# Where the first products of the second chunk's weights and the first maxima rows stand around a guard's branch

## The chip, the cores and the metric

The kernel runs on one core of a Trainium2 chip. The metric is the device time of one execution in microseconds (us); the time given for a kernel is the median of its runs. The profile is of one execution, taken by the hardware profiler; its times count from the first instruction. PE is the matrix engine (PEld its weight loads), DVE the vector engine, ACT the scalar engine, POOL the general one; SP only starts transfers here. A letter q behind an engine's name marks its instruction sequencer.

## The reference

One token block of 2048 rows and 512 columns goes through a layer norm; the result xn feeds two branches, and both are added to x.

```python
q = (xn @ wq) split in 32 heads of 16;  k = xn @ wk;  v = xn @ wv      # one shared key and value head
A = softmax(q k^T / 4) v, heads joined, @ wo

qB = einsum("nd,dhc->nhc", xn, w_q)                                  # 32 heads, 2 x 128 columns
s1, s2 = qB[..., :128] @ k1^T, qB[..., 128:] @ k2^T                     # 64 scores each
the two best of s1 and of s2 -> the two best of their four sums -> experts top_e, gates g
B = sum over heads and both experts of g * gelu(xn . u[top_e]) * v[top_e]   # 4096 experts
out = x + A + B
```

## The kernel before

The 32 expert heads are taken in 8 chunks of 4, the 2048 rows in 4 blocks of 512. For a chunk c, `wp_make(c)` (line 477) joins the query weights with the keys k1 and k2, so that one product with xn gives the scores: per head the raw weights are loaded by `wp_load(c, h)` (line 466), multiplied by the keys on PE into `pw` (line 487) and copied by ACT into `wt` (line 488); then four times four transposes `pwt` (line 494), a rounded high part by ACT (line 496) and the rest by DVE (line 497) make the tiles `wk`. `item` (line 513) multiplies them with xn into `psc` (line 531) and DVE finds the best entries. Blocks 0 and 1 then gather their experts' rows from HBM (`gather`, line 976, by POOL; `dot` and `add` on DVE); blocks 2 and 3 compute all experts densely (`dense`, line 656).

The attention runs in 32 units of four heads and 512 rows. `load_q(u)` (line 305) fills one of two tiles `qa`: for each of two pairs of heads three transfers of query rows, and one (line 314) of two rows of maxima, `d_m`, that are subtracted through the score product. `scores` (line 323) multiplies with the keys into `sc`, ACT takes the exponential into `pt` (line 330), and `pv` (line 338) multiplies by the values.

The maxima are normally zeros, which `zero_m` writes early. `guard` (line 251) bounds the largest score: DVE takes maxima, PE turns them (`pm`, line 258), DVE reduces, multiplies and compares (lines 260 to 264). Each engine then loads the flag into a register (line 265) and branches (line 266): only if the flag is set does `true_maxima` (line 269) compute the true ones. With these inputs it isn't set, and the block, which holds thousands of instructions, is jumped over.

Everything up to and including the guard is ordered by the framework's scheduler, which takes instructions by priority (their order in the program) as they become ready. The projections of this part use the pool `start`; when they are traced, `start_stack.close()` gives its space back and the pool `late` is opened in it (line 1251): the tiles `pt`, `e`, and the three buffers with the tag `gy`, which also take the raw weights from the third head of chunk 1 on. Buffers for the raw weights of that chunk's first two heads stand outside (lines 1249, 1250).

Behind the guard the order on every engine is written by hand. A loop over d (line 1259) calls `att_steps` for two of the 512 attention steps at a time: scores, values, `mid()` for the expert work of DVE and ACT, scores again, and `fill()`. `fill` draws work from the generator `score_thread` by `run_scores` (line 1130), which runs pieces and adds each one's planned cost to `spent[0]`, until a target is reached: 0.9 for a head's products (line 489), 0.45 for four transposes (line 500), three times `UNIT` (0.705) for a quarter of an item. The target of iteration d is line 1324. In the first iteration `att_steps` also loads the maxima rows of unit 0 and draws work ahead of the first scores (lines 1156 to 1158).

```python
aim = done0 + (FILL - done0) * (d + 1) / half if d < half else 1e6      # FILL 948, half 256
```

Of the kernel before, what the change touches and what calls it, by code (L numbers as in the profile page):

```python
# [49 lines left out]
HOLD = 44  # L50
MOST = 4.0
UNIT = 0.235


@with_exitstack
def tile_kernel(ctx, tc, x, wq, wkv, wo, wqT, kT, uv, ub, vb, out):
# [194 lines left out]
    def guard():  # L251

        mm = small.tile([P, 2], F32, name="mm", bufs=1)
        nc.vector.reduce_max(mm[:, 0:1], qmax, axis=AX.X)
        nc.vector.reduce_max(mm[:, 1:2], ksq_p, axis=AX.X)
        p = xtile("pm")
        for i in range(2):
            nc.tensor.transpose(p[:1, i * P:(i + 1) * P], mm[:, i:i + 1], ident)
        m2 = small.tile([1, 2], F32, name="m2", bufs=1)
        nc.vector.reduce_max(m2, p[:1, :2 * P].rearrange("p (a n) -> p a n", a=2), axis=AX.X)  # L260
        pr = small.tile([1, 1], F32, name="prd", bufs=1)
        nc.vector.tensor_mul(pr, m2[:, 0:1], m2[:, 1:2])
        fl = small.tile([1, 1], I32, name="flag", bufs=1)
        nc.vector.tensor_scalar(fl, pr, LIMIT2, None, op0=OP.is_gt)
        flag = nc.values_load(fl[0:1, 0:1], min_val=0, max_val=1)
        with tc.If(flag != 0):
            true_maxima()

    def true_maxima():
        ptile = lambda dt, shape: late[0].tile(list(shape), dt, name="mx", tag="pt", bufs=6)  # L270
# [34 lines left out]
    def load_q(u, rows=True, maxima=True):  # L305
        qb, hg = units[u]
        qa = qa_bufs[u % 2]
        QA[u] = qa
        c = slice(qb * 512, (qb + 1) * 512)
        for b in range(2):  # L310
            h0 = 4 * hg + 2 * b
            o = 64 * b
            if maxima:
                nc.sync.dma_start(raw(qa[o + 48:o + 50]), d_m[:, h0:h0 + 2, c])
            if rows:
                src = [d[h0 * DH:(h0 + 2) * DH, c].rearrange("(h r) n -> r h n", r=DH) for d in (d_qh, d_ql)]
                nc.sync.dma_start(raw(qa[o:o + 16]), src[0])
                nc.sync.dma_start(raw(qa[o + 16:o + 32]), src[0])
                nc.sync.dma_start(raw(qa[o + 32:o + 48]), src[1])
# [193 lines left out]
    def item(n_, ti, make=()):  # L513
# [15 lines left out]
        for k in range(KC):  # L529
# [6 lines left out]
            if k < KC - 1:  # L536
                yield 3 * UNIT
            if k == 1:
# [8 lines left out]
        if jb == BT - 1:  # L547
            batch(ph, c, b)
        yield 3 * UNIT

# [105 lines left out]
    def dense(DG, after):  # L656
# [81 lines left out]
        def first(b):  # L738
            p = xtile("pact")
            for k in activations(b, early[b], p):  # L740
                if k < KC - 1:
                    yield 3 * UNIT
            g, y = gate_rows(b), hh[:, b, :]
# [8 lines left out]
            LATER.append(go)  # L752
            yield 3 * UNIT

# [107 lines left out]
        def sums():  # L862
# [4 lines left out]
            for j in range(GT):  # L867
# [7 lines left out]
                nc.vector.tensor_add(acc, acc, p)  # L875
                yield 6 * UNIT

# [250 lines left out]
    spent = [0.0]  # L1128

    def run_scores(until=None, key=None):  # L1130
        while (until is not None and spent[0] < until) or (key is not None and key not in IDX):
            posts()
            try:
                cost = next(sgen)
            except StopIteration:
                spent[0] = 1e9
                posts()
                return
            if cost is None:

                if key is None:
                    return
                continue
            spent[0] += cost
# [4 lines left out]
    def att_steps(d, mid, fill):  # L1149
        i = 2 * d  # L1150
        run(STORES)
        if 144 <= i < STEPS and i % 128 == 16:
            PWO.extend((i // 128 - 1, j) for j in range(4))
        if i < STEPS:
            u, kc = divmod(i, 16)
            if i == 0:
                load_q(0, rows=False)
                run_scores(until=spent[0] + 1.8)
            if kc == 4 and u + 1 < 32:
                load_q(u + 1)  # L1160
            scores(u, kc, 0)
            scores(u, kc, 1)
        if 0 < i <= STEPS:
            pu, pk = divmod(i - 2, 16)
            pv(pu, pk)
            pv(pu, pk + 1)
            if pk == 14:
                unit_tail(pu)
        mid()
        if i < STEPS:  # L1170
            scores(u, kc + 1, 0)
            scores(u, kc + 1, 1)
        if out_ready() and (i % 128 >= HOLD and PWO[0][0] != 1 or i % 128 >= 32 and i % 4 == 0 and PWO[0][0] == 1):
            block_out()
            spent[0] += 3.6
        fill()

        pp, r = divmod(i, 32)
        if pp and pp < 16:
            if r == 4:  # L1180
                pair_load(pp - 1)
            if r == 6:
                pair_invert(pp - 1)
            if r == 10:
                pair_spread(pp - 1)
            if r == 12:
                pair_tail(pp - 1)
        if STEPS - 4 <= i <= STEPS:
            last_out_a((i - STEPS) // 2 + 2)
        if i == STEPS:  # L1190
            last_out_a(3)
        if i == STEPS + 2:
            last_out_b()
        if i >= 124 and i % 128 == 124 or i == STEPS - 30:
            lent[0] = 2
        if 128 <= i < STEPS and i % 128 == (26 if i // 128 == 2 else 10) or i == STEPS - 10:
            load_wo()
        if i == STEPS - 6:
            load_last()
# [49 lines left out]
    wp_load(1, 0)  # L1249
    wp_load(1, 1)  # L1250
    late[0] = pool("late", bufs=1)
    load_q(0, maxima=False)
    guard()
    E_ = mybir.EngineType
    with tc.manual_schedule(engines={E_.PE, E_.Activation, E_.DVE, E_.Pool, E_.SP}):
        done0 = spent[0]
        half = STEPS // 2
        pos, since = 0.0, half
        for d in range(half + 24):


            if dense_on[0] != 0:
                since = d
            if dense_on[0] == 1:
                pos += 2.6 if d < half * 3 // 4 else max(0.0, NSL - pos) / max(half - 3 - d, 1)
            else:
                pos += (2.1 if len(IDX) < NC * TPH else 2.3 if 0 <= d - since < 12 else 1.75, 0, 1.4, 1.5, 0.5)[dense_on[0]]

            todo = max(min(int(pos + 0.001), g_next[0]) - d_next[0], 0)

            def mid():
                post = POST[:]
                POST.clear()
                for act, _ in post:
                    act()
                tanhs(d_next[0])
                run(ON_ACT)
                ON_ACT.extend(LATER_ACT)
                LATER_ACT.clear()
                run(LAST)  # L1280
                LAST.extend(LATER)
                LATER.clear()
                rest = BEHIND[:]
                BEHIND.clear()

                dots(d_next[0] + todo - 1)
                if a_ready[0] > a_next[0]:
                    weigh(a_next[0] // SB)
                dots(d_next[0] + 1 if todo > 0 else 0)
                for _, fn in post:  # L1290
                    fn()
                sums = min(a_ready[0] - a_next[0], max(todo, 3) if d < half else 4)
                if dense_on[0] > 2:
                    sums = min(sums, 2)
                if quiet[0] > 0:
                    quiet[0] -= 1
                    sums = 0
                if dense_on[0] == 2:
                    run(CHAIN)

                def go():
                    n = sums
                    while rest or CHAIN or n > 0:
                        if n > 0:
                            adds(1)
                            n -= 1
                        elif not rest:
                            run(CHAIN)
                        if CHAIN:
                            CHAIN.pop(0)()  # L1310
                        if rest:
                            rest.pop(0)()
                    gathers(4)

                    for _ in range(1 if d < half - 4 else NT):
                        if OUTS:
                            experts_out(OUTS.pop(0))

                if dense_on[0] == 2:
                    POST_FILL.append(go)  # L1320
                else:
                    go()

            aim = done0 + (FILL - done0) * (d + 1) / half if d < half else 1e6

            def fill():
                run_scores(until=min(aim, spent[0] + MOST))
                run(POST_FILL)

            att_steps(d, mid, fill)  # L1330
        flush()
        run(STORES)
        while a_next[0] < NSL:
            dots(NSL)
            run(CHAIN)
            tanhs(d_next[0])
            adds(SB)
            run(STORES)
            gathers(NGB)
        assert not OUTS  # L1340
        run(STORES)
# [37 lines left out]
```

## Time and profile before

| | us |
|---|---|
| median of 3 runs (1899.36, 1899.49, 1910.27) | 1899.49 |
| the profiled execution, device time | 1905.66 |
| its span, first to last instruction | 1903.9 |

PE is busy in 95% of the span, DVE in 86%, ACT in 68%, POOL in 37%. In rows of the timeline the columns are the start, the duration, the engine, the line, the operation, the tiles written and read, the count of merged instructions, and in brackets the idle time before and who ended it. A duration of merged rows is that of the whole row. Rows of a group view give the shortest, the median and the longest duration in ns, and the first and last start. Rows of stretches give the stretch, its length, each engine's busy time with its number of instructions, the granted PE clock, the share of the DMA engines and GB/s.

### The profile page before, as it was taken

How to read it: one execution, taken by the hardware profiler on the slowest of the kernel's cores; microseconds unless marked ns; L12 is line 12 of the kernel's file. 1: busy time of each engine (PE TensorE's matmuls, PEld its weight loads, DVE VectorE, ACT ScalarE, POOL GpSimd, SP SyncE). 2: the span in 40 equal slices, each digit the busy share in tenths (PEclk: the TensorE clock that was granted, in tenths of full speed). 3: DMA queues.
4: the chain of work that ended last, by engine and by line, in shares of the span. 5: the costliest groups of instructions: out<-in, count | busy, mean ns of one | idle time of the engine just before them, and what ended most of it. 6: DMA issues, size and time to landing. Idle time of an engine off the chain costs nothing.

```text
span 1903.9 us, 35010 instructions
## 1 busy us (share of the span) xinstructions
PE 1817.4 (95%) x10990; PEld 957.9 (50%) x10990; DVE 1632.6 (86%) x6381; ACT 1290.6 (68%) x1803; POOL 697.3 (37%) x920
## 2 busy tenths in 40 slices
PE   6879999999999899999999999999998899999998
PEld 4544444555555344555555554555543355555553
DVE  6627788889998987999999898899989879999994
ACT  3236666655557887877887555555579877888874
POOL 1202334334443213344444345344532134444430
PEclk9989999999999999999999999999999999999999
DMA  7857878888773678799899987877736878899883
GB/s 267 318 187 245 287 264 299 290 291 284 233 264 102 222 234 264 250 282 294 269 284 301 371 290 246 289 247 262 240 111 227 263 224 291 274 281 289 275 278 102
DMA packets 245724, 489.76 MB, mean 257 GB/s; under 512 B 93972, under 2 KB 106644, under 8 KB 245532
## 3 DMA queue, kind: packets, MB, share of 16 engines
q0 software_dynamic: 73728, 268.47, 42.6%
q1 hardware_dynamic: 170568, 218.18, 35.0%
q8 instruction: 88, 1.44, 0.3%
q10 hardware_dynamic: 1236, 0.82, 0.1%
q14 instruction: 104, 0.85, 0.1%
HBM read 426.49 MB, written 55.61 MB: 253 GB/s over the span
## 4 chain that ended last, share of the span: by engine, by line
PE 74%; DVE 11%; DMA 3%; ACT 3%; issue 2%; SPq 0%; DVEq 0%; ACTq 0%; POOL 0%; POOLq 0%
PE pv L341 20%; PE psc L531 17%; PE sc L327 15%; PE pact L733 9%; PE pout L872 9%; DVE oh L792 3%; PE pwo L434 2%; DVE xa L1034 2%; DVE g L999 2%; ACT pt L330 2%; PE pw L487 2%; DMA wk<-dw 1%; DVE oh L795 1%; DVE i L546 1%; DVE oh L794 1%
## 5 line engine op out<-in xcount | busy, mean ns | idle before, releaser
L330 ACT ACTIVATE pt<-sc 128x1024 f32<-128x1024 f32 x1024 | 994.5, 1028 | 435.2 <-PE sc L327 384.7
L987 POOL DMA_INDIRECT g<-in_uv_dram,idx x512 | 559.0, 1092 | 988.9 <-DVE xa L1034 517.1
L341 PE MATMUL pv<-pt,vaug 128*32 128x512 f32 x4096 | 498.9, 605 | 0.0
L327 PE MATMUL sc<-qa,kaug 64*128 64x512 f32 x2048 | 388.4, 451 | 17.9 <-ACT pt L330 15.9
L531 PE MATMUL psc<-wk,xt 128*128 128x512 f32 x1536 | 388.9, 401 | 4.2 <-DVE wk L497 3.6
L1034 DVE SCALAR_TENSOR_TENSOR xa<-g,w,xa 128x512 f32<-128x512 f32 x512 | 372.5, 746 | 0.1
L999 DVE CUSTOM_DVE_ANT_0 g<-g,xa 128x512 f32<-128x512 f32 x512 | 336.0, 683 | 8.7 <-DMA g<-in_uv_dram,idx 8.3
L531 PEld LDWEIGHTS psc<-wk,xt 128*128 128x128 f32 x1536 | 277.7, 188 | 107.9 <-issue 41.2
L327 PEld LDWEIGHTS sc<-qa,kaug 64*128 64x128 f32 x2048 | 157.4, 185 | 335.5 <-ACT pt L330 218.2
L341 PEld LDWEIGHTS pv<-pt,vaug 128*32 128x32 f32 x4096 | 107.6, 110 | 246.8 <-issue 246.8
L546 DVE FIND_INDEX8 i<-m,psc 128x8 uint32<-128x64 f32 x1024 | 206.6, 223 | 0.0
L733 PE MATMUL pact<-xt,wk 128*128 128x512 f32 x768 | 195.9, 400 | 0.0
L872 PE MATMUL pout<-wk,wd 128*128 128x512 f32 x768 | 194.9, 402 | 0.2 <-DVE wd L930 0.2
L544 DVE MAX8 m<-psc 128x8 f32<-128x64 f32 x1024 | 146.7, 216 | 35.8 <-PE psc L531 28.3
L872 PEld LDWEIGHTS pout<-wk,wd 128*128 128x128 f32 x768 | 140.8, 188 | 47.5 <-DVE act L999 5.1
L733 PEld LDWEIGHTS pact<-xt,wk 128*128 128x128 f32 x768 | 139.4, 188 | 48.5 <-issue 17.5
L875 DVE TENSOR_TENSOR da<-da,pout 128x512 f32<-128x512 f32 x128 | 83.0, 681 | 9.9 <-PE pout L872 9.8
L698 DVE TENSOR_TENSOR wk<-rw,wk 128x512 fp32r<-128x512 f32 x128 | 85.0, 685 | 6.7 <-ACT wk L697 6.7
L792 DVE TENSOR_TENSOR oh<-oh 128x2048 f16<-128x2048 f16 x64 | 78.0, 1219 | 0.6 <-issue 0.4
L697 ACT CAST wk<-rw 128x512 fp32r<-128x512 f32 x128 | 74.1, 631 | 0.0
L546 DVE MATCH_VALUE_LOAD i<-m,psc 128x8 f32 x1024 | 73.8, 72 | 0.0
L590 POOL CAST fi<-i 128x64 f32<-128x64 uint32 x32 | 8.9, 278 | 148.9 <-DVE i L546 148.2
(159 smaller groups left out, 1350.0 us busy)
## 6 DMA issues: line engine op xcount, KB each, us to landing
wk<-dw SPq DMA_DIRECT2D x96, 512.0 KB
wqt<-in_wqT_dram SPq DMA_DIRECT2D x32, 512.0 KB
dw<-wk SPq DMA_DIRECT2D x32, 512.0 KB
rw<-in_ub_dram SPq DMA_DIRECT2D x64, 256.0 KB
rw<-in_vb_dram SPq DMA_DIRECT2D x64, 256.0 KB
gy<-dg SPq DMA_DIRECT2D x64, 256.0 KB
qa<-dqh SPq DMA_DIRECT2D x128, 64.0 KB
g<-in_uv_dram,idx POOLq DMA_INDIRECT x512
```

The source lines that it names most:

```text
L327: nc.tensor.matmul(p[:, b, :], kaug[o:o + 64, kc * P:(kc + 1) * P], QA[u][o:o + 64, i, :], start=True, stop=True)
L330: nc.scalar.activation(pt, p, AF.Exp, scale=SCALE)
L341: nc.tensor.matmul(PV[u][32 * j:32 * j + 32, :], vaug[:, kc, :], pt[:, b, :], start=kc == 0, stop=kc == 15)
L531: nc.tensor.matmul(p, XT[k][:, a, j * P:(j + 1) * P], WC[n_][k][:, bb, :], start=n == 0, stop=n == 11)
L544: nc.vector.max(m8[:, jb, s, :], p[:, s * E:(s + 1) * E])
L546: nc.vector.max_index(i8[:, jb, s, :], m8[:, jb, s, :], p[:, s * E:(s + 1) * E])
L733: nc.tensor.matmul(p, us[:, a, k * P:(k + 1) * P], XT[k][:, c, :], start=n == 0, stop=n == 11)
L792: nc.vector.tensor_tensor(out=oa, in0=num(P), in1=bc(0, tb, P), op=OP.is_equal)
L872: nc.tensor.matmul(p, wd[0][:, a, j * P:(j + 1) * P], vs[:, c, :], start=n == 0, stop=n == 5)
L987: nc.gpsimd.indirect_dma_start(out=gt, out_offset=None, in_=uv, in_offset=bass.IndirectOffsetOnAxis(ap=IDX[ph, c, ti][:, s:s + 1], axis=0))
L999: nc.vector.tensor_tensor_reduce(u, u, XN[TPH * ph + ti], scale=1.0, scalar=0.0, op0=OP.mult, op1=OP.add, accum_out=a[:, i:i + 1])
L1034: nc.vector.scalar_tensor_tensor(acc, v, w[:, i:i + 1], acc, op0=OP.mult, op1=OP.add)
```

## The change

The draw of work worth 1.8 planned us from `score_thread`, which stood ahead of the first scores in the hand-ordered loop, is made inside `guard`, between the comparison and the load of the flag. The maxima rows of unit 0 are loaded with its query rows, ahead of the guard, and once more inside the conditional block, behind `true_maxima`. `done0`, from which the targets of the loop start, is the counter less 1.8.

```diff
+FIRST = 1.8
...
         nc.vector.tensor_scalar(fl, pr, LIMIT2, None, op0=OP.is_gt)
+        run_scores(until=spent[0] + FIRST)
         flag = nc.values_load(fl[0:1, 0:1], min_val=0, max_val=1)
         with tc.If(flag != 0):
             true_maxima()
+            load_q(0, rows=False)
...
             u, kc = divmod(i, 16)
-            if i == 0:
-                load_q(0, rows=False)
-                run_scores(until=spent[0] + 1.8)
             if kc == 4 and u + 1 < 32:
                 load_q(u + 1)
...
-    load_q(0, maxima=False)
+    load_q(0)
     guard()
     E_ = mybir.EngineType
     with tc.manual_schedule(engines={E_.PE, E_.Activation, E_.DVE, E_.Pool, E_.SP}):
-        done0 = spent[0]
+        done0 = spent[0] - FIRST
```

## The prediction

> **What bounds the kernel now.** I read the page first, then the stretches, then the timeline around the guard, and last the lines of the branch and of the load of raw weights.
>
> ```profile
> span 1903.9 us, 35010 instructions
> PE 74%; DVE 11%; DMA 3%; ACT 3%; issue 2%; SPq 0%; DVEq 0%; ACTq 0%; POOL 0%; POOLq 0%
> ```
> ```profile
> 127.00:138.00 11.00, 5.27 (x16) 1.39 (x16) 0.00 (x0) 2.31 (x4) 0.00 (x0) 0.66 0.43 151
> 150.00:590.00 440.00, 432.47 (x2474) 223.87 (x2476) 383.70 (x2273) 271.94 (x348) 181.00 (x302) 1.00 0.79 268
> 730.00:1400.00 670.00, 668.82 (x3754) 361.55 (x3753) 612.47 (x2585) 455.62 (x605) 292.54 (x379) 1.00 0.83 273
> 1520.00:1880.00 360.00, 359.66 (x2013) 192.53 (x2011) 327.64 (x763) 280.19 (x393) 138.69 (x122) 1.00 0.85 266
> ```
> The chain that ended last is PE's in three quarters of the span, and behind 150 us PE idles 7.5 us of 440, 1.2 of 670 and 0.3 of 360. PE's work in these stretches does not change. So whatever the front loses or gains ahead of the loop's steady part reaches the end nearly in full. The front is another picture: between 127 and 138 us PE is busy 5.27 us of 11. There the whole chip waits for the guard:
>
> ```profile
> 118.07 3.69 PE L229 MATMUL pq<-xtt,wqs 128*128 128x512 f32 x15
> ...
> 123.55 0.44 SPq L319 DMA_DIRECT2D qa<-dql  x1
> ...
> 125.19 0.58 PE L258 MATMUL pm<-ident,mm 128*1 128x128 f32 x2 [0.97 <-DVE mm L254]
> ...
> 126.44 0.14 DVE L264 TENSOR_SCALAR flag<-prd 1x1 int32<-1x1 f32 x1
> 130.92 0.59 SPq L314 DMA_DIRECT2D qa<-dm  x2
> 131.31 0.33 PEld L487 LDWEIGHTS pw<-wqt,kTs 128*64 128x64 f32 x4 [6.04 <-PEq L266]
> 131.34 3.53 PE L487 MATMUL pw<-wqt,kTs 128*64 128x512 f32 x8 [5.57 <-PEq L266]
> 131.62 5.59 SPq L471 DMA_DIRECT2D wqt<-in_wqT_dram  x4
> ...
> 135.69 0.23 PEld L487 LDWEIGHTS pw<-wqt,kTs 128*64 128x64 f32 x4 [2.36 <-PE pw L487]
> 135.72 1.08 PE L487 MATMUL pw<-wqt,kTs 128*64 128x512 f32 x4 [0.86 <-PE pw L487]
> ...
> 136.73 0.73 PE L327 MATMUL sc<-qa,kaug 64*128 64x512 f32 x4
> ...
> 136.84 0.59 ACT L488 COPY wt<-pw 128x512 f32<-128x512 f32 x1 [1.35 <-PE pw L487]
> 137.45 1.28 ACT L330 ACT_TABLE_LOAD   x1
> 138.74 3.77 ACT L330 ACTIVATE pt<-sc 128x1024 f32<-128x1024 f32 x4
> ...
> 139.82 0.49 PE L327 MATMUL sc<-qa,kaug 64*128 64x512 f32 x2 [2.35 <-ACT pt L330]
> ```
> ```profile
> L265 PEldq TENSOR_LOAD <-flag x1: 492/492/492, 126.6 to 126.6; - x1
> L265 ACTq TENSOR_LOAD <-flag x1: 474/474/474, 126.6 to 126.6; - x1
> ```
> ```profile
> L266 ACTq COMPARE_BRANCH  x1: 50/50/50, 127.1 to 127.1; - x1
> L266 SPq COMPARE_BRANCH  x1: 50/50/50, 127.2 to 127.2; - x1
> L266 PEldq COMPARE_BRANCH  x1: 3808/3808/3808, 127.2 to 127.2; - x1
> L266 DVEq COMPARE_BRANCH  x1: 72/72/72, 127.2 to 127.2; - x1
> L266 DVEq EVENT_SEMAPHORE  x1: 21/21/21, 130.3 to 130.3; - x1
> ```
> The flag is there at 126.58 (126.44 + 0.14). PE loads it in 0.49, stands 3.81 in its branch, and begins its next weights at 131.31: 4.7 us from the flag load. Then come four records per head: eight (two heads) in 3.53, a gap, and four more (a third head). The first scores start at 136.73, the table load for the exponential at 137.45 behind the third copy, the first exponential at 138.74, and PE's third pair of scores waits for it. That exponential is where the front ends: its start is what I follow.
>
> **How many heads move.** The counter stands at 16.68 when the guard is reached: chunk 0 costs 4 x 0.9 + 4 x 0.45 + 16 x 0.705. Two heads bring it to 16.68 + 0.9 + 0.9, which in binary floating point is just below 18.48, so a third head is drawn. The twelve records ahead of 136.73 say the same of the kernel before. In the changed kernel, too, three heads stand ahead of the branch, and the third needs weights that the first two don't.
>
> ```profile
> L471 SPq DMA_DIRECT2D wqt<-in_wqT_dram x2: 386/747/1108, 53.0 to 63.5; - x2
> ```
> ```profile
> L471 SPq DMA_DIRECT2D wqt<-in_wqT_dram x3: 419/464/992, 131.6 to 133.1; - x3
> ```
> The first row (40 to 127 us) is the loads for heads one and two, started at 53.0 and 63.5; the second (127 to 136.5) starts with the third head's.
>
> **The change, part by part.** *Heads one and two.* Their weights are in place by about 67.6 (63.5 and the 4.07 worked out below), so the scheduler may put them into any idle place of PE, at the latest behind `pm`, from 125.77. PE is at full speed there, where the third head's 1.08 is the row for a head: 2 x 1.08 = 2.2, done by 127.9 at the latest, at best at no cost under the 4.0 us between the end of the last `pq` row (121.76) and `pm`, which only small products break. In the kernel before they took 3.53, at a low clock.
>
> *The third head.* Its buffer lies in space that the projections hold. The last `pq` ends at 121.76 and SP's last transfer of the projection part is issued by 123.99. So I bound its issue between 121.8 and 126.6 (SP's own flag load) and take 124.5, just behind that last transfer. Before, it was issued at 131.62 and its first weights were read at 135.69: 4.07. So the product starts at 128.6 and ends at 129.7 (1.08 more); bounds 127.9 + 1.08 = 129.0, or 126.6 if the first two are hidden, and 126.6 + 4.07 + 1.08 = 131.8. This is a wait that the change adds: PE's flag load and branch are queued behind it, and on ACT the copy, with ACT's flag load, branch and table load.
>
> *PE's branch.* It costs the same 4.7 us from the flag load: 129.7 + 4.7 = 134.4 for the first scores instead of 136.73, 2.3 earlier (bounds 131.3 to 136.5). [...]
>
> *ACT.* The third copy ends at 129.7 + 0.1 + 0.59 = 130.4, the flag load takes 0.47, the branch 0.05. How long ACT then fetches no row of ACT shows: DVE's next instruction came 3.1 behind its branch (127.2 to 130.3), PE needed 3.8. I take 3.1: 134.0. The table load of 1.28 then runs while PE makes the first scores, instead of behind a copy: 135.4. The first scores (134.4 plus about 1.0) are there by then. So the first exponential starts at 135.4 instead of 138.74: 3.3 earlier. With the early bound, scores at 131.3 and an exponential at 132.4, it is 6.3; with the late one, 136.5 + 1.0, it is 1.2.
>
> *The clock.*
> ```profile
> 126.62:131.30 4.68, 0.00 (x0) 0.00 (x0) 0.00 (x0) 0.00 (x0) 0.00 (x0) 0.50 0.04 11
> 131.30:136.80 5.50, 4.60 (x14) 1.16 (x14) 0.00 (x0) 1.17 (x2) 0.00 (x0) 0.70 0.67 231
> ```
> In the branch the granted clock falls to 0.50, and the products that followed took 3.53/2 = 1.77 a head against 1.08. These products brought the clock back ahead of the scores; now the scores come first and pay: four records in 0.73 become 1.46. My 1.0 for the first pair of banks holds that. [...]
>
> *The transfers.* The maxima rows (0.59 of SP) and three raw loads (0.42 to 0.99 each) go ahead of SP's flag load, where SP is idle from 123.99 to 126.6; I cost them at nothing. If that cover is gone SP's branch comes up to 2 us later, and the next thing that needs SP, the store of the new weights, comes only behind the first subtraction:
> ```profile
> 144.76 0.69 DVE L497 TENSOR_TENSOR wk<-pwt,wk 128x512 fp32r<-128x512 f32 x1 [18.18 <-ACT wk L496]
> ```
> The extra load inside the block isn't executed. DVE and POOL have nothing new in front of their branches.
>
> *The targets.* `done0` becomes 19.38 - 1.8 = 17.58 instead of 16.68, as three heads were drawn. The target of d = 0 is 21.21 instead of 20.32, so it draws three groups of transposes instead of one, and the score work stays up to 0.9 planned us ahead of the attention, fading to nothing at d = 255. No work is added; its order changes by about one piece per iteration.
>
> **Sum.** 3.3 us, in the terms of the profiled execution 1905.66 - 3.3 = 1902.4. That execution lies 6.2 (0.3%) above the median of the runs shown; against the median I forecast 1899.49 - 3.3 = 1896.2, with the bounds 1893 to 1898.
>
> **Rivals.** (a) *All three products under the guard*: the third load is issued at 121.8 and the first two products are hidden; PE reaches the flag in time, the scores start at 131.3, the exponential at 132.4. Then 6.3 are gained: 1893.2. Against it: SP's queue still has stores and query rows to start until 123.99.
>
> (b) *Nothing gained*: the third load comes late. The exponential starts at issue + 4.07 + 1.08 + 4.7 + 1.0 by way of PE; that is 138.74 for an issue at 127.9, which is behind SP's own flag load at 126.6. From there on each us later costs one. Against it: nothing in the trace holds SP between 124 and 126.6. About 1899.5.
>
> (c) *Slower, by the new order in the dense stages.* PE idles most where it waits in lockstep for DVE's one-hot tiles and for the exponential:
> ```profile
> 596.00:730.00 134.00, 118.46 (x1127) 53.48 (x1127) 114.92 (x241) 116.13 (x188) 30.90 (x32) 0.96 0.68 218
> 1402.00:1536.00 134.00, 115.33 (x1118) 52.76 (x1121) 117.23 (x245) 115.73 (x188) 32.09 (x30) 0.96 0.68 216
> ```
> ```profile
> PE pg L825 <- DVE oh L795: 12.2, 12, 1.6
> PE sc L327 <- ACT pt L330: 4.6, 10, 1.5
> ```
> The two stretches hold the same work and idle 15.5 and 18.7 us, 3.2 apart, by their place in the order alone (the waits shown are the second's). If score pieces that come earlier push the one-hot products ahead of DVE, these 34 us grow; at 10% more the front's gain is gone, and at two thirds more (23 us) the kernel is over 1% slower. For it: the targets are shifted by a whole piece in the first dense stage (0.9 x 0.73 at d = 68). Against it: the shift has nearly faded in the second (0.2 at d = 190), and PE's steady stretches have no slack to lose. I price it at 1899 to 1912, near 1904 (half as much idle again in the first stage, 7.8, less 3.3).
>
> (d) *Faster by the same order*: the first stage could lose idle time too; 1885 to 1891.
>
> **Chances.** Forecast with its bounds 0.62, (a) 0.08, (b) 0.07, (c) 0.16, (d) 0.07. The range leaves out the far ends of (c) and (d): 1888 to 1904. About 1% (19 us) is what a measurement of this kernel can tell from no change. The front alone can't gain that, as all it holds between the flag and the first exponential is 12.2 us. Only the order could move 19 us either way: faster 0.06, within 1% 0.83, slower 0.11.
>
> **What would show it.** Right: three products and copies of `wt` ahead of PE's and ACT's branch; PE's flag load held behind the third, near 129.7; the scores at 134.4 as the first work behind the branch at a low clock; the first exponential near 135.4; no idle of DVE or PE beyond 150 us that wasn't there. Wrong: a first exponential at or behind 138.7; or one that is earlier while the dense stretches idle by more than the 15.5 and 18.7 us.

## The result, and the profile after

The changed kernel takes 1914.12 us (median of 8 runs, 1908.59 to 1918.26). The kernel before, run beside it, takes 1906.93 (8 runs, 1899.36 to 1910.27). The ratio is 1.0044 with a 95% interval of 1.0031 to 1.0057: about 8.4 us slower, where 3.3 us faster was forecast. That is within 1%, the likeliest class, but on the other side and outside the range. Of the 17.9 us between 1896.2 and 1914.12, 7.4 are the base: the kernel before stood at 1906.93 in this comparison and not at 1899.49. The other 10.5 are the 3.3 that were forecast and the 7.2 by which the two medians differ.

The profiled execution of the changed kernel took 1915.46 us. Its page, span and chain of waits:

```profile
span 1913.7 us, 35010 instructions
...
PE 73%; DVE 15%; ACT 2%; DMA 2%; issue 1%; SPq 0%; DVEq 0%; ACTq 0%
```

The chain is still PE's, with DVE's share up from 11% to 15%. The span is 9.8 us longer than before's 1903.9. To find where, I read the stretches of the changed kernel that answer to those shown of before, each moved 4.9 to 5.3 us later:

```profile
131.89:142.89 11.00, 3.42 (x14) 1.00 (x10) 0.00 (x0) 2.06 (x4) 0.00 (x0) 0.70 0.58 197
155.29:595.29 440.00, 431.43 (x2468) 222.56 (x2467) 382.84 (x2269) 272.29 (x348) 182.48 (x302) 1.00 0.79 268
601.29:735.29 134.00, 114.53 (x1115) 53.50 (x1113) 114.71 (x241) 115.09 (x188) 31.83 (x34) 0.99 0.66 215
735.29:1405.29 670.00, 668.03 (x3762) 360.69 (x3761) 610.07 (x2575) 456.77 (x605) 287.44 (x374) 1.00 0.83 273
1407.29:1541.29 134.00, 116.61 (x1107) 53.74 (x1107) 115.63 (x243) 114.64 (x187) 33.14 (x36) 0.95 0.66 214
1525.29:1885.29 360.00, 358.49 (x1997) 192.22 (x1999) 327.30 (x763) 278.35 (x393) 136.56 (x122) 1.00 0.84 264
```

PE's idle time is the length less the second number. Behind the front it is 8.6 us (before 7.5), 19.5 (15.5), 2.0 (1.2), 17.4 (18.7) and 1.5 (0.3). It is more in four of the five stretches, and most of the added idle time (4 us) is in the third row, the first dense stage. The granted clock there is 0.99 where it was 0.96, and 0.03 of 134 us is 4.0 us: by this estimate PE made its products there sooner and waited for the rest. The guard, in the timeline of the changed kernel:

```profile
130.57 0.38 PE L259 MATMUL pm<-ident,mm 128*1 128x128 f32 x2 [0.98 <-DVE mm L255]
...
130.88 1.94 PE L490 MATMUL pw<-wqt,kTs 128*64 128x512 f32 x8
...
131.22 5.39 SPq L474 DMA_DIRECT2D wqt<-in_wqT_dram  x4
...
131.61 0.14 DVE L265 TENSOR_SCALAR flag<-prd 1x1 int32<-1x1 f32 x1
...
135.12 1.08 PE L490 MATMUL pw<-wqt,kTs 128*64 128x512 f32 x4 [2.31 <-issue]
...
141.45 1.42 PE L330 MATMUL sc<-qa,kaug 64*128 64x512 f32 x4 [5.25 <-SPq L268]
142.59 1.28 ACT L333 ACT_TABLE_LOAD   x1 [5.76 <-PE sc L330]
143.88 2.94 ACT L333 ACTIVATE pt<-sc 128x1024 f32<-128x1024 f32 x3
```

And the sequencers' rows at the flag load, the branch and the wait for the third head's weights, from the groups of these lines:

```profile
L267 PEldq TENSOR_LOAD <-flag x1: 490/490/490, 135.1 to 135.1; - x1
...
L268 SPq EVENT_SEMAPHORE  x8: 17/17/17, 140.8 to 141.4; - x8
...
L268 PEldq COMPARE_BRANCH  x1: 3948/3948/3948, 135.7 to 135.7; - x1
L268 SPq COMPARE_BRANCH  x1: 50/50/50, 136.7 to 136.7; - x1
...
L490 PEldq EVENT_SEMAPHORE  x6: 51/51/3916, 130.6 to 135.0; - x6
...
L333 ACTq EVENT_SEMAPHORE  x13: 17/38/1122, 141.0 to 145.8; - x13
```

The instruction queues among the DMA queues between 135.7 and 141.5 us (queue, packets, MB, share of the 16 engines); between 105 and 135.6 they move nothing:

```profile
q8 instruction: 2, 0.03, 2.3%
q14 instruction: 4, 0.03, 1.5%
```

All three products are in front of the branch. But the flag comes at 131.75 instead of 126.58, and from the flag to the first exponential it takes 12.13 us (143.88 - 131.75) where it took 12.16 (138.74 - 126.58). From there to the end it takes 1769.9 instead of 1765.2. So the 9.8 us of the profiles fall into three parts, and each has to be explained by itself: the front 5.2 later, the guard no shorter, and 4.7 more behind it (parts rounded).

Three things in the rows were not in the forecast. The first scores wait for SP ("<-SPq L268"): SP branches at 136.7, a microsecond behind PE, and behind its branch makes eight semaphore steps of 17 ns, from 140.8 to 141.4. And the last of the four raw loads in SP's row starts at about 136.2, when PE's third product has ended and a buffer comes free (131.22 + 5.39, less the load's own 0.4); SP's branch stands behind it in the same queue. The first of the four, which brings the third head's weights, was held as well. SP's queue shows it among its waits from 120 to 140 us (who waited, for whom, us in total, times, longest):

```profile
SPq L474 <- DMA dql<-qt: 1.1, 1, 1.1
```

SP had issued its last transfer of the projections by 129.8, but the load then stood 1.1 us until a store of projected queries had landed.

### The profile page after: what moved, and what is told of

It is laid out like the page before. It is cut to its first block, busy times and chain, and to the rows that moved or that the text cites. A ratio compares the mean times of both kernels' runs of the same rounds, so it can differ in the third digit from the quotient of the medians.

```text
span 1913.7 us, 35010 instructions
## 1 busy us (share of the span) xinstructions
PE 1820.7 (95%) x10990; PEld 960.0 (50%) x10990; DVE 1630.9 (85%) x6381; ACT 1292.1 (68%) x1803; POOL 694.2 (36%) x920
## 4 chain that ended last, share of the span: by engine, by line
PE 73%; DVE 15%; ACT 2%; DMA 2%; issue 1%; SPq 0%; DVEq 0%; ACTq 0%
PE pv L344 20%; PE psc L534 17%; PE sc L330 14%; PE pact L736 9%; PE pout L875 8%; DVE oh L795 4%; DVE xa L1037 3%; DVE g L1002 2%; PE pwo L437 2%; PE pw L490 1%; DVE oh L798 1%; DVE oh L797 1%; DVE i L549 1%; ACT pt L333 1%; DMA dinv<-rc 1%
## 5 line engine op out<-in xcount | busy, mean ns | idle before, releaser
L990 POOL DMA_INDIRECT g<-in_uv_dram,idx x512 | 552.6, 1079 | 979.6 <-DVE xa L1037 500.2
L330 PE MATMUL sc<-qa,kaug 64*128 64x512 f32 x2048 | 387.9, 451 | 18.9 <-ACT pt L333 13.2
L330 PEld LDWEIGHTS sc<-qa,kaug 64*128 64x128 f32 x2048 | 157.3, 185 | 335.8 <-ACT pt L333 230.9
L736 PEld LDWEIGHTS pact<-xt,wk 128*128 128x128 f32 x768 | 139.7, 188 | 47.6 <-issue 17.1
L549 DVE MATCH_VALUE_LOAD i<-m,psc 128x8 f32 x1024 | 69.0, 67 | 0.0
```

The lines of the kernel that those rows point to most:

```text
L330: nc.tensor.matmul(p[:, b, :], kaug[o:o + 64, kc * P:(kc + 1) * P], QA[u][o:o + 64, i, :], start=True, stop=True)
L549: nc.vector.max_index(i8[:, jb, s, :], m8[:, jb, s, :], p[:, s * E:(s + 1) * E])
L736: nc.tensor.matmul(p, us[:, a, k * P:(k + 1) * P], XT[k][:, c, :], start=n == 0, stop=n == 11)
L990: nc.gpsimd.indirect_dma_start(out=gt, out_offset=None, in_=uv, in_offset=bass.IndirectOffsetOnAxis(ap=IDX[ph, c, ti][:, s:s + 1], axis=0))
```

## The experiments

All are compared with the kernel before on the same chip. Microseconds worked out from a ratio are the ratio less one, times that comparison's median of before (1905 to 1911). Three marks read from each timeline go with them: the end of the comparison that makes the flag, the start of the first scores, and the start of the first exponential. They are of one execution each. The way from flag to exponential is 11.83 to 13.07 us in the three kernels of the table that leave the guard as it was (before, rows alone, targets alone), so half a microsecond there tells nothing.

| kernel | ratio, 95% interval | flag | first scores | first exponential | flag to exponential | exponential to end |
|---|---|---|---|---|---|---|
| before | | 126.58 | 136.73 | 138.74 | 12.16 | 1765.2 |
| changed | 1.0044 [1.0031, 1.0057] | 131.75 | 141.45 | 143.88 | 12.13 | 1769.9 |
| rows alone | 1.0014 [1.0001, 1.0027] | 129.70 | 139.53 | 141.53 | 11.83 | 1762.7 |
| products and targets | 1.0010 [0.9996, 1.0024] | 126.01 | 135.16 | 137.72 | 11.71 | 1768.1 |
| targets alone | 1.0031 [1.0018, 1.0044] | 124.19 | 135.00 | 137.26 | 13.07 | 1769.6 |
| two products, old targets | 1.0001 [0.9986, 1.0017] | 123.95 | 132.71 | 135.14 | 11.19 | 1767.5 |
| changed, no rows | 1.0041 [1.0026, 1.0056] | 127.25 | 136.35 | 138.75 | 11.50 | 1780.8 |
| changed, old targets | 1.0010 [0.9993, 1.0027] | 132.39 | 142.94 | 145.37 | 12.98 | 1764.6 |
| two products, no rows, old targets | 0.9984 [0.9970, 0.9998] | 129.92 | 135.45 | 137.96 | 8.04 | 1767.1 |
| three products, no rows, old targets | 0.9990 [0.9972, 1.0008] | 129.53 | 139.69 | 142.02 | 12.49 | 1764.0 |

In the kernels with "no rows", the maxima rows of unit 0 aren't loaded unless the flag is set: the zeros of the cleared tile are used.

**The rows alone.** To the kernel before:

```diff
         with tc.If(flag != 0):
             true_maxima()
+            load_q(0, rows=False)
...
             if i == 0:
-                load_q(0, rows=False)
                 run_scores(until=spent[0] + 1.8)
...
-    load_q(0, maxima=False)
+    load_q(0)
```

> Only the maxima rows of unit 0 are loaded ahead of the guard, and again inside the skipped block; the products stay in the loop and the targets are those of before. Three theories. FRONT: the two row loads change the order that the scheduler gives the projections, and that costs the 5.2 us by which the flag came later in the changed kernel (126.58 to 131.75): then this kernel is 3 to 7 us slower than before, flag near 131, and the stretch from flag to first exponential stays near 12. GUARD: the cost comes from what stands ahead of the branch (products, loads): then this kernel equals before within 1 us. TARGETS: the cost comes from score work running ahead in the loop: within 1 us of before too.

Measured: 1.0014, about 2.7 us (0.2 to 5.1). What the edit does is seen far ahead of the guard. SP's queue in its timeline:

```profile
18.62 0.32 SPq L249 DMA_DIRECT2D dio<-g  x1
22.16 0.30 SPq L315 DMA_DIRECT2D qa<-dm  x1
24.96 0.61 SPq L209 DMA_DIRECT2D kaug<-kh  x1
```

The same place in the kernel before:

```profile
18.55 0.32 SPq L249 DMA_DIRECT2D dio<-g  x1
23.36 0.32 SPq L239 DMA_DIRECT2D dqh<-qt  x1
23.77 0.62 SPq L209 DMA_DIRECT2D kaug<-kh  x1
```

The scheduler doesn't put the load of the rows where it is written. It is ready as soon as the zeros are stored, so it goes in at 22.16. From there on SP's order is another (the first store of projected queries now stands behind the stores of the keys), and in a few places that of ACT, DVE and PE.

What this costs is seen between two products of the projections, `ksq_p` of the first and of the second 512 rows. In the timeline of the kernel before and of this one:

```profile
24.86 0.38 PE L214 MATMUL ksq_p<-ksq,blk 16*32 16x512 bf16 x1
...
37.56 0.38 PE L237 MATMUL pqs<-qsq,blk 128*32 128x512 bf16 x1 [1.17 <-ACT qsq L236]
...
43.47 0.38 PE L214 MATMUL ksq_p<-ksq,blk 16*32 16x512 bf16 x1
```
```profile
26.50 0.38 PE L214 MATMUL ksq_p<-ksq,blk 16*32 16x512 bf16 x1
...
40.66 0.38 PE L237 MATMUL pqs<-qsq,blk 128*32 128x512 bf16 x1 [2.63 <-ACT qsq L236]
...
48.09 0.38 PE L214 MATMUL ksq_p<-ksq,blk 16*32 16x512 bf16 x1
```

From the one `ksq_p` to the other it is 18.6 us before and 21.6 here: 1.5 more up to `pqs`, where PE waits longer for ACT, and 1.5 more behind it. The 73 products that start in between are the same. In the fourteen profiles it is 18.6 to 19.0 us in the eleven without the rows ahead, and 21.6, 21.6 and 22.2 in the three with them.

**The products and the targets, rows where they were.**

```diff
+        run_scores(until=spent[0] + FIRST)
         flag = nc.values_load(fl[0:1, 0:1], min_val=0, max_val=1)
...
-                run_scores(until=spent[0] + 1.8)
...
-        done0 = spent[0]
+        done0 = spent[0] - FIRST
```

> Only the three products are moved ahead of the branch, with the changed targets; the maxima rows are loaded behind the branch as before. FRONT: the flag is back near 126.6 and the kernel is no slower than before (0 to -3 us). GUARD: flag near 126.6, first exponential 11 to 13 us behind it because the third head's weights hold PE's branch, so no gain: 0 to +1 us. TARGETS: 2 to 4 us slower than before, with flag and first exponential as before and the loss behind 150 us.

Measured: 1.0010, an interval that holds 1. The flag is back at 126.01, but the way from the flag to the exponential is still 11.71. Here the scores wait for something else, in the timeline of this kernel:

```profile
135.16 1.55 PE L329 MATMUL sc<-qa,kaug 64*128 64x512 f32 x4 [5.14 <-DMA qa<-dm]
```

**The targets alone.**

```diff
-        done0 = spent[0]
+        done0 = spent[0] + 0.9
```

> Only the targets of the loop are moved: done0 is 17.58 instead of 16.68, nothing else. TARGETS: 2 to 4 us slower than before, all of it behind 150 us. FRONT and GUARD: within 1 us of before.

Measured: 1.0031, about 5.9 us (3.4 to 8.4). One constant, with no instruction added, carries the larger part of the loss.

**Two products, old targets, rows behind.** As the products above, with

```diff
+FIRST = 1.79
...
+        done0 = spent[0] - 1.8
```

so that two heads are drawn, neither needs the late weights, and the targets are those of before.

> Two heads' products ahead of the branch instead of three, targets as before, maxima rows behind the branch as before. GUARD: with no wait for the third head's weights PE's flag load follows the second product, about 128, PE is back near 132.7, scores and table load follow: first exponential 2 to 4 us earlier than before and the kernel 2 to 4 us faster. FRONT: 2 to 4 us faster as well, as the front keeps its order. TARGETS: as before, so equally faster; a result that isn't faster speaks against all three.

Measured: 1.0001. The gain didn't come. PE branches at once, 0.6 us behind the flag, and is out of its branch about 128.9; then, in the timeline:

```profile
129.94 0.60 SPq L316 DMA_DIRECT2D qa<-dm  x2
...
132.71 1.42 PE L329 MATMUL sc<-qa,kaug 64*128 64x512 f32 x4 [6.42 <-DMA qa<-dm]
...
136.22 0.80 PE L329 MATMUL sc<-qa,kaug 64*128 64x512 f32 x2 [2.09 <-ACT pt L332]
```

The maxima rows, issued at 129.94 behind SP's own branch, are now the last to come: the scores start 2.8 us later. In the kernel before they were issued at 130.92, PE made its products from 131.34 to 136.80, and the scores at 136.73 didn't wait for the rows: the products behind the branch were their cover, and moving the products alone takes it away.

**The changed kernel without the row load.**

```diff
-    load_q(0)
+    load_q(0, maxima=False)
```

> The changed kernel without the load of the maxima rows ahead of the guard: unit 0's rows keep the zeros that the tile was cleared to at the start, and are loaded only inside the skipped block. FRONT: the projections have the order of before again, the flag comes at 124 to 127 instead of 131.75, and the kernel is 4 to 6 us faster than the changed one, so 2 to 5 us slower than before because of the targets. If the rows' order is not the cause, the flag stays near 131.

Measured: 1.0041. The flag comes back to 127.25, but the time doesn't follow: 1780.8 us from the first exponential, 11 more than any other kernel of the table. One place where it loses, in its timeline:

```profile
1061.40 0.96 PE L875 MATMUL pout<-wk,wd 128*128 128x512 f32 x3 [0.54 <-DVE wd L933]
1063.86 0.80 PE L875 MATMUL pout<-wk,wd 128*128 128x512 f32 x1 [1.50 <-DVE wd L933]
1064.59 1.22 PE L330 MATMUL sc<-qa,kaug 64*128 64x512 f32 x4
1065.73 3.64 PE L344 MATMUL pv<-pt,vaug 128*32 128x512 f32 x16
...
1073.43 0.74 PE L330 MATMUL sc<-qa,kaug 64*128 64x512 f32 x4
```

and in DVE's rows just ahead of it:

```profile
1057.22 0.35 DVE L382 RECIPROCAL rc<-rc 128x32 f32<-128x32 f32 x1 [2.00 <-DMA rc<-dsum]
```

DVE stands 2.00 us for the denominators to come back from HBM, what PE needs comes behind that in DVE's order, PE stands 0.54 and 1.50, and then its scores take 1.22 instead of 0.74 and its values 3.64 where the changed kernel has 1.92. The stretches show the granted clock (the number ahead of the last two):

```profile
1060.00:1064.00 4.00, 1.97 (x8) 1.00 (x6) 3.81 (x7) 0.62 (x1) 2.79 (x3) 0.94 1.02 417
1064.00:1070.00 6.00, 6.00 (x25) 1.74 (x25) 4.07 (x12) 1.94 (x2) 1.54 (x2) 0.50 1.03 413
```

So at this place the stall is paid twice: 2.04 us of standing, and at the granted clock of 0.50 another 2.2 in these scores and values (0.48 and 1.72). It isn't so at every stall of this kernel: behind one of 1.50 that ends at 1011.26 the next scores take 0.73, at a granted clock of 1.00 (1012 to 1016). In the changed kernel PE stands 0.79 at this place, and the next scores take 0.73. Against the kernel with the same targets and the rows behind the branch, it falls back in steps like this at some six places between 740 and 1240 us; at two of them DVE waits for a transfer, at others PE waits up to 0.9 for an exponential. Why they are in this kernel alone is open.

**The changed kernel with the old targets.**

```diff
-        done0 = spent[0] - FIRST
+        done0 = spent[0] - 2.7
```

> The changed kernel with the targets of before (done0 is 16.68). TARGETS: the stretch from the first exponential to the end is back at about 1765 us (1769.9 in the changed kernel, 1769.6 with the targets alone), and the kernel is 3 to 5 us faster than the changed one; the flag stays near 130 to 132. Otherwise the stretch stays near 1769.

Measured: 1.0010 (0.9993 to 1.0027), and 1764.6 us from exponential to end, the value of before. Undoing the constant takes 8.4 us to about 1.9; the late flag (132.39) and the long guard (12.98) stay.

**Two products, no rows, old targets.** The last two edits together, with `FIRST = 1.79` and `done0 = spent[0] - 1.8`.

> No row load ahead or behind the branch, two heads' products ahead of it, targets of before. FRONT, GUARD and TARGETS together: flag at 124 to 127; PE is out of its branch 5 us later and, with no third head and no rows to wait for, starts the first scores at once; table load, first exponential 7.5 to 8.5 us behind the flag instead of 12.2. One more product stands behind it (1 us). 3 to 5 us faster than before. If the first scores still start 8 us or more behind the flag, something else holds PE.

Measured: 0.9984 (0.9970 to 0.9998), about 3 us faster. From the flag to the exponential it takes 8.04 us, 4.1 less than before. In its timeline:

```profile
135.45 1.49 PE L330 MATMUL sc<-qa,kaug 64*128 64x512 f32 x4 [2.72 <-PEq L268]
136.66 1.28 ACT L333 ACT_TABLE_LOAD   x1 [3.31 <-PE sc L330]
137.96 2.94 ACT L333 ACTIVATE pt<-sc 128x1024 f32<-128x1024 f32 x3
```

With neither the late weights nor a transfer in the way, the scores wait for PE's own branch alone.

**Three products, no rows, old targets.** The kernel before with the three products ahead, no rows, and `done0 = spent[0] - 2.7`.

> As the kernel without the row load, three products ahead of the branch, but with the targets of before. TARGETS: 3 to 5 us faster than with the changed targets; against before 0 to 2 us faster, by what the guard gains with three products (flag to first exponential 10.5 to 12).

Measured: 0.9990 (0.9972 to 1.0008), and 12.49 us from flag to exponential. The third head alone takes back what two gain. In the groups of this kernel's lines:

```profile
L268 SPq COMPARE_BRANCH  x1: 50/50/50, 134.9 to 134.9; - x1
L268 ACTq COMPARE_BRANCH  x1: 50/50/50, 135.0 to 135.0; - x1
```

and its scores in the timeline:

```profile
139.69 1.31 PE L330 MATMUL sc<-qa,kaug 64*128 64x512 f32 x4 [5.30 <-SPq L268]
```

SP and ACT branch 5.4 us behind the flag (129.53), held by the third head's weights, product and copy, and by a fourth raw load that waits for that product's buffer; with two heads SP branches at 130.5, 0.6 behind the flag. By the loop of `wp_make` the calls for the first three heads bring three loads. The fourth belongs to the fourth head, which the program draws behind the guard. In the kernel with the products and targets, where the row load stands behind the branch, it is issued behind SP's branch, at 134.19; in those with three products and no row load there, it stands ahead of it. I take that to be the scheduler's doing; no run shows it.

**How the targets act.** Three more kernels move only the constant of the kernel before, in the manner of the targets alone: by -0.9, +0.45 and +1.8.

> The kernel before with done0 lower by 0.9, so the score work stays up to 0.9 planned us further behind the attention than before. Theory of the shift (being ahead costs in itself, so much per planned us; +0.9 cost 5.9 us): the mirror image, 3 to 6 us faster than before. Theory of the chance (each shift deals the same work out anew, and the order of before is one draw that fell well): not faster, between 1 faster and 8 slower. In the second case PE's idle time behind the first scores, 51 to 54 us in the profiles with the old targets and 57 to 63 with the new ones, grows or stays; in the first it falls below 50.

> The kernel before with done0 higher by 0.45, half the shift of the changed kernel. Theory of the shift: about half of 5.9, 2 to 4 us slower. Theory of the chance: anything from 1 faster to 8 slower, not in proportion; PE's idle time behind the first scores between 51 and 63 us, with the place of the added idle another than with 0.9.

> The kernel before with done0 higher by 1.8, twice the shift of the changed kernel. Theory of the shift: about twice 5.9, 10 to 14 us slower. Theory of the chance: 0 to 9 slower; a result at or below the 5.9 of the half shift speaks for it.

| shift of `done0` | ratio, 95% interval | us |
|---|---|---|
| -0.9 | 1.0043 [1.0027, 1.0059] | +8.2 |
| 0 | 1 | 0 |
| +0.45 | 1.0004 [0.9990, 1.0017] | +0.8 |
| +0.9 | 1.0031 [1.0018, 1.0044] | +5.9 |
| +1.8 | 1.0087 [1.0069, 1.0105] | +16.6 |

The theory of the shift falls with the first row: being behind costs as well. PE's idle time behind the first scores, the sign that was named for the theory of the chance, is 60.4, 58.4 and 61.5 us for -0.9, +0.45 and +1.8, against 52.7 before, and so speaks for chance; but the last row lies outside its 0 to 9. What the five show: half a head's product changes nothing that can be measured, a whole one in either direction costs 6 to 8 us, and two cost 17. Whether that is a valley, or four orders that fell worse than the one of before, five points don't tell.

Where it costs is seen when the time is added up by iterations of the loop (from the first scores of one iteration to those of another; us, with PE's idle time behind the stroke):

| iterations | before | rows alone | changed, old targets | three, no rows, old | changed | products and targets | targets alone |
|---|---|---|---|---|---|---|---|
| 0 to 29 | 225.0 / 11.2 | 225.9 / 10.4 | 226.4 / 9.0 | 224.7 / 9.1 | 226.9 / 10.8 | 226.9 / 10.8 | 227.4 / 10.8 |
| 60 to 83 | 144.3 / 14.6 | 142.7 / 17.1 | 142.9 / 15.3 | 144.1 / 16.4 | 143.8 / 19.5 | 143.8 / 19.5 | 143.8 / 21.0 |
| 84 to 177 | 655.1 / 2.1 | 654.5 / 1.8 | 656.2 / 3.1 | 654.5 / 1.8 | 655.6 / 2.0 | 655.1 / 1.8 | 656.0 / 2.9 |
| 178 to 209 | 201.5 / 18.7 | 200.8 / 18.5 | 200.8 / 20.3 | 201.5 / 17.5 | 203.7 / 18.0 | 202.4 / 20.3 | 202.4 / 20.4 |
| 210 to end | 334.3 / 6.1 | 333.9 / 5.8 | 333.9 / 5.8 | 334.5 / 6.3 | 335.4 / 6.7 | 335.7 / 7.0 | 335.4 / 6.7 |

(30 to 59: 206.9 to 207.0 in all.) The last three columns have the new targets. In the mean they lose 1 to 2 us in each of three places: the first thirty iterations, 178 to 209 with the second dense stage, and the rest. In iterations 60 to 83, the first dense stage, PE idles 4 us more and yet they take no longer: the stage's pace isn't set by PE's work, and what PE saves there comes back as idle time.

About half of the loss in the first thirty isn't one: with the new targets three score products more (a quarter of an item, 0.7 planned us) are made there, and three fewer in iterations 60 to 83. The rest is not idle time of PE, which is no longer there than in the kernel before, and none of its waits explains it: for the chunk's weights it stands 2.6 us in the changed kernel over these iterations and 3.6 in the kernel before. For the two late places I found no single wait either. So the loss is shown to come from the targets, and how it arises stays open.

**The table load.** The last run adds one exponential of a single element to the best kernel, ahead of the loop:

```diff
+        warm = small.tile([1, 1], F32, name="warm", bufs=1)
+        nc.scalar.activation(warm, ident[0:1, 0:1], AF.Exp)
         done0 = spent[0] - 1.8
```

> As the kernel without the row load, with two products ahead and the old targets (8.04 us from flag to first exponential, ratio 0.9984), and one exponential of a single element as ACT's first work behind its branch, which brings the table load there. Theory of the table (the 1.28 us stands exposed because the load waits in ACT's order behind the first scores, and is hidden once something ahead of it asks for the table): table load ahead of the first scores, flag to first exponential 6.5 to 7.0, the time 0.2 to 0.3% below the kernel before (1 to 2 us below the one without it). Rival (the first scores, at half clock, come no earlier than the exponential does now, or the table is loaded late because ACT comes out of its branch behind PE): flag to first exponential 7.7 to 8.3, no change against 0.9984.

It didn't test what it was for. ACT's rows in its timeline:

```profile
10.89 1.28 ACT L1257 ACT_TABLE_LOAD   x1
12.19 0.20 ACT L1257 ACTIVATE warm<-ident 1x1 f32<-1x1 f32 x1
...
135.63 1.28 ACT L333 ACT_TABLE_LOAD   x1 [3.70 <-PE sc L330]
136.93 3.85 ACT L333 ACTIVATE pt<-sc 128x1024 f32<-128x1024 f32 x4
```

The exponential ran at 12.19, in the projections, and the table was loaded again at 135.63, 1.14 behind the start of the first scores, as in the changed kernel (8.43 us from flag to exponential). The time is nevertheless the best of the study: 1906.14 against 1910.85, ratio 0.9972 (0.9956 to 0.9988), 5.4 us faster than before. What it adds to the 3.1 of the kernel without it lies within the two intervals.

## Why the prediction was wrong, step by step

**Right.** Three heads stand ahead of the branch. The first two are made right behind `pm`, in 1.94 us at a granted clock of 1.00, where 2.2 was the latest case. (The full speed that the prediction took there was not that of the kernel before, where the granted clock was 0.50 over `pm`, from 125.10 to 125.80.) The third's product starts 3.9 behind the issue of its weights (131.22 to 135.12; forecast 4.07). PE's branch takes 3.95; it takes 3.81 in the kernel before, with no product in front, 4.37 and 4.73 in two kernels with two (no rows, old targets, without and with the table load), and 4.15 to 4.43 in three more with three (old targets; products and targets; no rows, old targets). So no product in front of the branch covered it here, as the sum, which took over the 4.7 in full, had it. The prediction says of ACT that it fetches there; what the traces show is that the instruction queues moved six packets from 135.7 to 141.5 in the changed kernel and none in the thirty microseconds ahead, and five from 126.6 to 131.3 in the kernel before. The first scores pay the low clock with 1.42 (forecast 1.46): the granted clock was 0.50 from 141.40 to 142.90, and in the kernel before, where the same four take 0.73, it was 1.00 (136.70 to 137.50). The 1.77 to 1.08 a head that the prediction names is a factor of 1.6; over those first two heads the granted clock was 0.50 up to 134.30 and 0.86 in the microsecond behind. The second pair was slow too, for which the sum had nothing: in the changed kernel its four records take 1.71 from 144.96 on, at a granted clock of 0.50, and two of them take 0.80 in the kernel with two products and the rows behind, and 0.49 in the kernel before.

**Wrong in the guard: 8.8 us forecast from flag to exponential, 12.13 measured.** Three steps of the working, one after another, make up the 3.3:

- *"The third head"*: its product was to end 3.1 behind the flag (129.7 - 126.58) and ended 4.5 behind it (136.20 - 131.75). The load was put at 124.5, two microseconds ahead of the flag and just behind SP's last transfer; it was issued at 131.22, half a microsecond ahead of the flag. It had to wait until a store of the projections had landed, not only until the last transfer was issued. 1.3 lost.
- *"The transfers"*, costed at nothing because SP was idle. The bound given, SP's branch "up to 2 us later", was far too small (4.9 behind the flag, against 0.6 before), and "the next thing that needs SP" was not the store of the new weights: PE's scores wait for semaphore steps that SP makes behind its branch. Scores 5.25 behind the third product's end instead of 4.7: 0.55 lost. Two things lie in it: PE loads the flag at 135.1, while its third product still runs, and is out of its branch at 139.7, 3.5 behind that product's end; then it stands 1.7 until SP has made its steps.
- *"ACT"*: "The table load of 1.28 then runs while PE makes the first scores." The table load began 1.14 behind the start of the first scores (0.72 in the kernel before), so from scores to exponential it is 2.43 and not 1.0: 1.4 lost. In the changed kernel ACT is out of its branch at 141.0, 4.2 behind it where 3.1 was taken, and then stands 1.12 in one wait ahead of the load, which the timeline puts down to the scores ([5.76 <-PE sc L330]). That a table asked for ahead of this wait would be hidden is not shown; the run that should have shown it missed.

Rival (b), nothing gained, had the guard's outcome with one of the three causes.

**Wrong ahead of the guard.** "The transfers" looked only at the place where the row load is written. The scheduler started it at 22 us, and the projections got another order. The flag comes at 129.70 to 132.39 in the three kernels with the rows ahead and at 123.95 to 129.92 in eleven without (means 131.3 and 126.7); those without spread by 6 us although nearly all of them have the same order up to the guard, so one flag says little. The stage between the two `ksq_p` says more: 3.0 to 3.6 us longer in all three with the rows ahead and in no other. By time, the rows alone cost 2.7 us (0.2 to 5.1), and the old targets with and without them differ by 1.0010 to 0.9990. Sign and size agree in these; in the pair with the new targets (1.0044 with the rows, 1.0041 without) the gain doesn't show, as the kernel without them loses elsewhere. In the profile of the changed kernel some of the 5.2 lies ahead of the first instruction that differs, where its input tiles landed 0.8 us later, and is no effect of the change.

**Wrong behind the guard: the step "the targets".** "No work is added; its order changes by about one piece per iteration", costed at nothing, is the largest miss: 5.9 us (3.4 to 8.4) alone, and 6.5 of the 8.4 go when it alone is undone. Rival (c) had this cause and its sign, with a chance of 0.16. Its place was wrong in the main: the first dense stage idles more, as it said, but takes no longer, while the iterations with the second one, where the shift has nearly faded, lose 1 to 2 us, and so do the opening and the end.

The parts add up within the noise: rows 2.7, targets 5.9, three products (measured with no row load at all) -1.9 (-5.3 to 1.5), together 6.7 against 8.4 (5.9 to 10.9). Other pairs give other sizes: the targets cost 6.5 between the two kernels with the rows ahead, and 9.7 between the two with three products and no rows. Each figure is good to about 3 us.

## What to carry to other kernels

Before work is moved in front of a branch, ask of each engine in turn, the one that only starts transfers too, what the moved work puts in front of its own branch (here PE, out of its own, stood 1.7 us until SP had made its steps); move only the part whose inputs are certain to be there (two heads gained 4 us of the guard, the third gave it all back). Work behind a branch may be the cover of a transfer that is issued there, and moving it alone can then gain nothing (1.0001); here the gain came when that transfer was left out, and two products with the rows ahead and the old targets were not tried. A transfer that is ready early may be started early wherever it is written (the rows at 22.16 us), and then it changes the order of what it passes. A change of a constant that only sets when filler work is drawn is a change of the whole order of the kernel, and the constant is best held fixed while something else is tried, and swept by itself.

## What the runs showed of the hardware that wasn't expected

- Behind its branch SP makes eight semaphore steps on the guard's line, of 17 ns each; from the first to the last it is 0.5 to 0.6 us in seven kernels (before, changed, products and targets, changed with the old targets, and the three with no rows and old targets, one of them with the table load). In the changed kernel another engine waits for them: PE left its branch at about 139.7 and began at 141.45. What the steps are for no run shows.
- ACT's load of the exponential's table took 1.28 us and began behind the start of the first scores: 0.72 us in the kernel before, 1.14 in the changed one, and 1.14, 1.21 and 1.14 in those with two products (rows behind; no rows; no rows and the table load). In these four with products ahead of the branch ACT had been idle for 5.76, 6.93, 3.31 and 3.70 us ahead of it.
- Two stalls of PE of 0.54 and 1.50 us within four, of which it was busy 1.97, were followed by 6 us at a granted clock of 0.50, in which matmuls took 1.6 to 1.9 times as long (1.22 to 0.74, 3.64 to 1.92), in the kernel without the row load; behind a stall of 1.50 at another place of it the clock was 1.00. In the kernel before the clock was 0.50 over `pm` (125.10 to 125.80), in the branch, where PE did nothing for 4.7 us, and over the first products behind it (131.30 to 134.30).
- While engines stood in their branches the instruction queues moved packets: six from 135.7 to 141.5 in the changed kernel, none from 105 to 135.6; five from 126.6 to 131.3 in the kernel before, none from 105 to 126.5. What they brought no run shows.
